# Tiles of one head pair in the attention of a fused kernel: the ninth tile alone, with zeros multiplied at the start and buffers of their own for the last output halves

## The chip, the cores and the metric

The kernel runs on one core of a Trainium2 chip. The metric is the device time of one execution in microseconds, the median of several runs. The core has a matrix engine (TensorE, PE in the profile; its weight loads are shown apart as PEld), a vector engine (VectorE, DVE), an activation engine (ScalarE, ACT), a general engine (GpSimd, POOL) and a queue engine (SyncE, SP) that issues transfers (DMA). The engines run side by side, each through its own instructions in order, and wait for each other by semaphores. SBUF is the working memory with 128 partitions; PSUM is the memory into which TensorE writes.

## The reference

Attention over 8 batches of 8 heads, 576 rows, head dimension 64, in which all scores more than tau below the row's largest are dropped, and then a two-layer network without biases whose nonlinearity is h - tanh(h).

```python
def _attn_ref(q, k, v, tau):                 # q, k, v: (8, 8, 576, 64), tau = 0.02
    scores = (1.0 / np.sqrt(64)) * np.matmul(q, k.transpose(0, 1, 3, 2))
    thresh = np.max(scores, axis=-1, keepdims=True) - tau
    scores = np.where(scores >= thresh, scores, -1000000000.0)
    scores = scores - np.max(scores, axis=-1, keepdims=True)
    attn = np.exp(scores)
    attn = attn / (np.sum(attn, axis=-1, keepdims=True) + 1e-09)
    return np.matmul(attn, v)

def _moe_ref(x, w_in, w_out):                # x: (4608, 512), w_in: (512, 2048), w_out: (2048, 512)
    h = x @ w_in
    g = h - np.tanh(h)
    return g @ w_out

# x is the attention's output, with the heads of one row side by side
```

## The kernel before

Two heads are worked on together as a *pair*; there are 32 pairs, four to a batch. A pair has nine tiles of 128 query rows: four of the first head, four of the second, and one that takes the last 64 rows of both. The program counts tiles through from 0 to 287 and takes one step for each. In a step it computes the scores of the tile eight ahead, shifts and bends the scores of tiles further on, turns one tile's weights (transposes them and takes the exponential), multiplies another's with v, and puts in a piece of the network on a batch that is already attended to.

Two neighbouring tiles are a *duo*: an A and a B, side by side in one buffer of 2 x 576 columns, that is nine blocks of 128. As a pair has nine tiles, the before kernel counts A and B straight through all the pairs. The ninth tile of an even pair is the A of a duo whose B is the shared tile of the next pair, which there comes first:

```python
def kind(i):
    return "AB"[i % 2]

def place(i):
    p, j = divmod(i, TPP)                    # TPP = 9
    j = j - p % 2
    return (p, None, 4) if j in (-1, 8) else (p, j // 4, j % 4)
```

Scores, and their copy to SBUF with the row maximum. The buffer in PSUM is one of two:

```python
def scores(i):
    p, hh, t = place(i)
    ps = ps_big.tile([P, 1024], F32, name="psS", tag="big")
    ...
    if hh is None:                           # rows of both heads: eight matmuls, 64 rows each
        ...
    else:
        lhs = qT[:, (5 * hh + t) * P : (5 * hh + t + 1) * P]
        for n, kk in enumerate((kT, kS)):
            for dst, src in ((main, MAIN[hh]), (rem, REM[hh])):   # 512 and 64 columns
                nc.tensor.matmul(out=ps[:, dst], lhsT=lhs, rhs=kk[:, src],
                                 start=(n == 0), stop=(n == 1))
    sc = sc_pool.tile([P, S], F32, name="sc")
    ...
    nc.vector.tensor_scalar(out=sc, in0=ps[:, lo : lo + S], scalar1=SC, scalar2=None,
                            op0=ALU.mult, op1=ALU.max, accum_out=mx[:, c : c + 1])
```

Once in a duo the maxima are turned into the biases of both tiles. A Prelu with a very steep slope then drops what lies below the threshold. From the seventh pair on, a duo is transposed by a DMA; the first six pairs are transposed on TensorE:

```python
def shift(i):
    if kind(i) == "A":
        return
    ...
    nc.vector.tensor_scalar(out=..., in0=..., scalar1=-1.0, scalar2=tau, op0=ALU.mult, op1=ALU.add)
    nbs[i - 1], nbs[i] = nb[:, 0:1], nb[:, 1:2]

def kink(i):
    ...
    nc.scalar.activation(out=z, in_=sc, func=ACT.Prelu, bias=nb, scale=1.0, alpha=STEEP)
    if on_pe(i):                             # pairs 0 to 5
        zts[i] = zt
    elif kind(i) == "B":
        zts[i] = zt_pool.tile([P, TPP, P], BF16, name="zT")
        nc.sync.dma_start_transpose(out=zts[i], in_=zt)

def weights(i):                              # the branch for pairs 6 to 31
    ...
        pt = p_pool.tile([P, TPP * P], FP16, name="pT")
        nc.scalar.activation(out=pt[:, 0 : n * P], in_=zts.pop(i)[:, 0:n, :], func=ACT.Exp)
```

The weighted sum of a duo. The fifth block holds the last 64 columns of A above the first 64 of B, and one matmul of 130 columns serves both. The two shared tiles in one duo belong to two pairs and are multiplied one pair at a time:

```python
def attend(i):
    ...
    nc.tensor.matmul(out=po[:, t - 1 : t + 1, :], lhsT=pt[:, 4 * P : 5 * P],
                     rhs=vb[:, hh, 4:6, :], start=True, stop=False, ...)
    for n in range(8):
        ab, c = divmod(n, 4)
        blk = 5 * ab + c
        nc.tensor.matmul(out=po[:, t - 1 + ab, :], lhsT=pt[:, blk * P : (blk + 1) * P],
                         rhs=vb[:, hh, c, :], start=False, stop=(n == 7), ...)

def attend_shared(p, ab, pt):                # five matmuls of 130 columns
    for n in range(5):
        blk, c = ((5 * ab + n, n) if n < 4 else (4, 4 + ab))
        nc.tensor.matmul(out=ops[p, 1 - p % 2][:, 4:6, :], lhsT=pt[:, blk * P : (blk + 1) * P],
                         rhs=vb[:, :, c, :], start=(n == 0), stop=(n == 4))
```

The output tiles come from a pool that goes round two buffers. The last row block of the last part is done in two halves of 256 columns, from the same two buffers, so that the stores of the first half can begin earlier:

```python
y_pool = pool("y", 2)

def project(m, ms, part, ps, last, cols=slice(0, d_model)):
    ...
        yo = y_pool.tile([P, nc_], F32, name="yo")
        if last:
            nc.scalar.copy(out=yo, in_=ps)
        else:
            nc.vector.tensor_copy(out=yo, in_=ps)
    # the store of yo is issued after that; for the last part two stores of 64 rows
```

The start: k and q of pair 0 are loaded in pieces, split into a high and a low half on ScalarE, VectorE and GpSimd, and transposed on TensorE. Until the first of them has landed TensorE has nothing to do. GpSimd splits k and q of the later pairs, casts v, makes the shifted copy kS of each kT, and casts the 16 pieces of the two weight matrices in the first seven pairs.

Of the kernel before, what the change touches and what calls it, by code (L numbers as in the profile page):

```python
# [18 lines left out]
def kernel(  # L19
# [27 lines left out]
    NPAIR = B * HPAIR  # L47
    DM_C = d_model // P
    DF_C = d_ff // P


    TPP = 9
    NTILE = NPAIR * TPP

# [16 lines left out]
    NMB = B + 1  # L71

    const = ctx.enter_context(tc.tile_pool(name="const", bufs=1))
    ident_f16 = const.tile([P, P], FP16, name="ident_f16")
    make_identity(nc, ident_f16)
    ident_bf = const.tile([P, P], BF16, name="ident_bf")
# [10 lines left out]
    for i in range(NV):  # L87
        vb = const.tile([P, 2, 6, D + 1], BF16, name=f"vb{i}")
        nc.gpsimd.memset(vb[:, :, 4:6, :], 0.0)
        nc.gpsimd.memset(vb[:, :, 0:4, D : D + 1], 1.0)  # L90
        nc.gpsimd.memset(vb[0:64, :, 4, D : D + 1], 1.0)
        nc.gpsimd.memset(vb[64:P, :, 5, D : D + 1], 1.0)
        vbs.append(vb)


    mx3 = []
# [71 lines left out]
    warm = const.tile([P, 1], F32, name="warm")  # L168
    nc.vector.memset(warm, 0.0)
    nc.scalar.activation(out=warm, in_=warm, func=ACT.Exp)  # L170

    hls = {}

# [109 lines left out]
    REM = (slice(512, 576), slice(576, 640))  # L283
    scs, mxs, nbs, zs, zts, pts, ops = {}, {}, {}, {}, {}, {}, {}

    def kind(i):

        return "AB"[i % 2]

    def place(i):  # L290

        p, j = divmod(i, TPP)
        j = j - p % 2
        return (p, None, 4) if j in (-1, 8) else (p, j // 4, j % 4)

    def scores(i):
        p, hh, t = place(i)
        qT, kT, kS = mats[p, "q"], mats[p, "k"], mats[p, "ks"]
        ps = ps_big.tile([P, 1024], F32, name="psS", tag="big")
        main, rem, lo = slice(0, 512), slice(512, 576), 0  # L300
        if kind(i) == "B":
            main, rem, lo = slice(512, 1024), slice(448, 512), 448
        if hh is None:
            qrem = REM
            if q_by_dma(p):
                qrem = (slice(512, 640, 2), slice(513, 640, 2))
            for n, kk in enumerate((kT, kS)):
                for dst, srcs in ((main, MAIN), (rem, REM)):
                    for hh in range(2):
                        nc.tensor.matmul(  # L310
                            out=ps[64 * hh : 64 * hh + 64, dst],
                            lhsT=qT[:, qrem[hh]], rhs=kk[:, srcs[hh]],
                            start=(n == 0), stop=(n == 1),
                        )
        else:
            lhs = qT[:, (5 * hh + t) * P : (5 * hh + t + 1) * P]
            for n, kk in enumerate((kT, kS)):
                for dst, src in ((main, MAIN[hh]), (rem, REM[hh])):
                    nc.tensor.matmul(  # L319
                        out=ps[:, dst], lhsT=lhs, rhs=kk[:, src],  # L320
                        start=(n == 0), stop=(n == 1),
                    )
        sc = sc_pool.tile([P, S], F32, name="sc")
        if kind(i) == "B":
            mx = mxs[i] = mxs.pop(i - 1)
        else:
            mx = mxs[i] = mx3[i // 2 % len(mx3)]
        c = int(kind(i) == "B")
        nc.vector.tensor_scalar(  # L329
            out=sc, in0=ps[:, lo : lo + S], scalar1=SC, scalar2=None,  # L330
            op0=ALU.mult, op1=ALU.max, accum_out=mx[:, c : c + 1],
        )
        scs[i] = sc

    def shift(i):

        if kind(i) == "A":
            return
        mx = mxs.pop(i)
        nb = st_pool.tile([P, 9], F32, name="nb", tag="nb")  # L340
        nc.vector.tensor_scalar(  # L341
            out=nb.rearrange("p (a b) -> p a b", b=3)[:, :, 0:2],
            in0=mx.rearrange("p (a b) -> p a b", b=4)[:, :, 0:3],
            scalar1=-1.0, scalar2=tau, op0=ALU.mult, op1=ALU.add,
        )
        nbs[i - 1], nbs[i] = nb[:, 0:1], nb[:, 1:2]

    def kink(i):
        sc, nb = scs.pop(i), nbs.pop(i)
        if kind(i) == "B":  # L350
            zt = zs.pop(i - 1)
            z = zt[:, S:W]
        else:
            zt = zs[i] = z_pool.tile([P, W], BF16, name="z")
            z = zt[:, 0:S]
        nc.scalar.activation(  # L356
            out=z, in_=sc, func=ACT.Prelu, bias=nb, scale=1.0, alpha=STEEP
        )
        if on_pe(i):
            zts[i] = zt  # L360
        elif kind(i) == "B":
            zts[i] = zt_pool.tile([P, TPP, P], BF16, name="zT")
            nc.sync.dma_start_transpose(out=zts[i], in_=zt)

    def weights(i):


        kd = kind(i)
        n, off = {"A": (4, 0), "B": (5, 4)}[kd]
        if on_pe(i):  # L370
            z = zts.pop(i)
            pl, tag = (ps_h, "h") if i % 2 and i < HPAIR * TPP else (ps_y, "y")
# [23 lines left out]

    def attend(i):

        if kind(i) == "A":
            return  # L400
        p, hh, t = place(i)
        vb, pt = vbs[p % NV], pts[i]
        if hh is None:

            attend_shared(p - 1, 0, pt)
            return
        if t == 1:
            ops[p, hh] = ps_o.tile([P, 6, D + 1], F32, name="psO", tag="o")
            if p % 2 and hh == 0:
                attend_shared(p, 1, pts.pop(i - 2))  # L410
        po = ops[p, hh]

        nc.tensor.matmul(  # L413
            out=po[:, t - 1 : t + 1, :], lhsT=pt[:, 4 * P : 5 * P],
            rhs=vb[:, hh, 4:6, :], start=True, stop=False, skip_group_check=True,
        )
        for n in range(8):
            ab, c = divmod(n, 4)
            blk = 5 * ab + c
            nc.tensor.matmul(  # L420
                out=po[:, t - 1 + ab, :], lhsT=pt[:, blk * P : (blk + 1) * P],
                rhs=vb[:, hh, c, :], start=False, stop=(n == 7), skip_group_check=True,
            )
        pts.pop(i)

    def attend_shared(p, ab, pt):

        vb = vbs[p % NV]
        for n in range(5):
            blk, c = ((5 * ab + n, n) if n < 4 else (4, 4 + ab))  # L430
            nc.tensor.matmul(
                out=ops[p, 1 - p % 2][:, 4:6, :], lhsT=pt[:, blk * P : (blk + 1) * P],
                rhs=vb[:, :, c, :], start=(n == 0), stop=(n == 4),
            )

    osb = {}

    def norm(p, hh):
        po = ops.pop((p, hh))
        if hh == 0:  # L440
            osb[p] = o_pool.tile([P, 5, 2, D], BF16, name="osb")
        shared = hh != p % 2
        n = 4 + shared
        rc = st_pool.tile([P, 5], F32, name="rc", tag="rc")
        nc.vector.reciprocal(out=rc[:, 0:n], in_=po[:, 0:n, D])
        nc.vector.tensor_tensor(  # L446
            out=osb[p][:, 0:4, hh, :], in0=po[:, 0:4, 0:D],
            in1=rc[:, 0:4].unsqueeze(2).to_broadcast([P, 4, D]), op=ALU.mult,
        )
        if shared:  # L450
            nc.vector.scalar_tensor_tensor(
                out=osb[p][:, 4, :, :], in0=po[:, 4:6, 0:D], scalar=rc[:, 4:5],
                in1=own, op0=ALU.mult, op1=ALU.mult,
# [56 lines left out]
    def project(m, ms, part, ps, last, cols=slice(0, d_model)):  # L510
# [4 lines left out]
            )  # L515
        if part == 3:
            nc_ = cols.stop - cols.start
            yo = y_pool.tile([P, nc_], F32, name="yo")
            if last:
                nc.scalar.copy(out=yo, in_=ps)  # L520
            else:
# [157 lines left out]
    for s in range(-AHEAD, NTILE + LAG + 3):  # L679
# [37 lines left out]
        for i in atts.pop(s, []):  # L717
            pp, jj = divmod(i, TPP)
            if i < NTILE:
                attend(i)  # L720
                odd = pp % 2
                if jj == 3 + odd:
                    norm(pp, 0)
                elif odd and jj in (0, 8):
                    norm(pp - (jj == 0), 1)
            if pp and jj == 1 + pp % 2:
                emit_x(pp - 1)
        for step in plan.pop(s, []):
            step()
# [61 lines left out]
```

## Time and profile before

| | |
|---|---|
| time, median of 3 runs | 540.55 us (540.01 to 540.85) |
| span of the profiled execution | 538.8 us, granted TensorE clock 1.00 |
| TensorE matmul busy | 508.4 us, 94% |
| VectorE busy | 424.5 us, 79% |
| ScalarE busy | 435.2 us, 81% |
| GpSimd busy | 290.2 us, 54% |
| scores copy, L329, 288 times | 753 ns each |
| Prelu, L356, 288 times | 770 ns each |
| Exp of a duo, L392, 117 times | 1153 ns each |
| transposes of z by DMA, L363, 117 times | 3.6 us from issue to landing |
| first matmul on loaded data | 5.42 us from the start |

A group in the profile is all instructions of one line, engine and shape. Its busy time counts overlapping instructions once, and the mean is that of one instruction from its beginning to its end, so neighbours that overlap make the mean larger than the distance between them. A row of the waits reads: who waited, for whom, us in total, how many times, the longest. The chain of work goes back from the last instruction to what released it, and so on to the start. The numbers after L are lines of the kernel.

### The profile page before, as it was taken

What the parts mean: (1) busy time and instruction counts of PE and PEld (TensorE: products, weight loads), DVE (VectorE), ACT (ScalarE), POOL (GpSimd) and SP (SyncE); (2) the same over time, 40 slices, a digit from 0 to 9 for tenths busy, and PEclk for the clock granted to TensorE, in tenths of its full rate; (3) what the DMA queues carried; (4) which work ended last, traced back from release to release, by engine and by line L of the source; (5) the groups of instructions that cost most, each with busy time, mean ns of one, the idle gap of its engine ahead of it and who ended that gap; (6) DMA issues with size and microseconds to landing.
All of it is one profiled execution on the core that took longest, in us unless ns stands there. A gap on an engine that the chain in (4) does not pass through costs nothing.

```text
span 538.8 us, 12796 instructions
## 1 busy us (share of the span) xinstructions
PE 508.4 (94%) x4640; PEld 289.0 (54%) x4640; DVE 424.5 (79%) x1183; ACT 435.2 (81%) x617; POOL 290.2 (54%) x390
## 2 busy tenths in 40 slices
PE   5989899989999999999999899999999999999996
PEld 3666566555555555555555555555455555444444
DVE  4898888988888988888888888898889788554440
ACT  4999899998888998899888988899888989543330
POOL 7999996776555656666645654566665620000000
PEclk9999999999999999999999999999999999999999
DMA  6555657989898999798989889798978986301113
GB/s 209 174 184 151 205 177 141 195 181 183 162 196 157 181 182 199 155 180 183 196 175 183 184 182 189 159 166 195 191 164 176 202 140 116 103 19 41 39 40 79
DMA packets 202687, 85.32 MB, mean 158 GB/s; under 512 B 170240, under 2 KB 195072, under 8 KB 202624
## 3 DMA queue, kind: packets, MB, share of 16 engines
q1 hardware_dynamic: 202032, 84.08, 74.4%
q8 instruction: 36, 0.59, 0.5%
q10 hardware_dynamic: 592, 0.43, 0.3%
q14 instruction: 27, 0.22, 0.1%
HBM read 36.70 MB, written 9.44 MB: 86 GB/s over the span
## 4 chain that ended last, share of the span: by engine, by line
PE 64%; DVE 12%; ACT 8%; POOL 5%; DMA 5%; issue 4%; SPq 1%; DVEq 0%; ACTq 0%; POOLq 0%
PE psY L512 19%; PE psH L486 17%; PE psS L319 14%; ACT z L356 3%; PE psO L420 3%; DVE g L505 3%; DVE sc L329 3%; PE psHt L486 3%; DVE kT L251 2%; ACT pT L392 2%; PE psS L310 2%; PE ps_k L228 2%; DMA qT<-qhl 2%; DVE yo L522 2%; DMA zT<-z 2%
## 5 line engine op out<-in xcount | busy, mean ns | idle before, releaser
L356 ACT ACTIVATE z<-sc,nb 128x576 bf16<-128x576 f32 x288 | 216.9, 770 | 39.0 <-DVE nb L341 38.5
L329 DVE TENSOR_SCALAR_CACHE_REDUCE sc<-psS 128x576 f32<-128x576 f32 x288 | 214.2, 753 | 40.5 <-PE psS L319 29.0
L512 PE MATMUL psY<-w_out_sb,g 128*128 128x512 bf16 (+1 forms) x592 | 145.9, 373 | 0.8 <-DVE yo L522 0.8
L257 POOL COPY kS<-kT 64x1152 f16<-64x1152 f16 x62 | 70.7, 1141 | 131.9 <-DVE kT L251 69.7
L392 ACT ACTIVATE pT<-zT 128x1152 f16<-128x1152 bf16 x117 | 134.9, 1153 | 2.1 <-DMA zT<-z 2.1
L486 PE MATMUL psH<-xT,w_in_sb 128*128 128x512 bf16 x480 | 123.3, 379 | 2.5 <-DVE g L505 2.3
L319 PE MATMUL psS<-kT,qT 128*128 128x512 f16 (+1 forms) x512 | 104.9, 286 | 9.7 <-DVE kT L251 4.9
L319 PEld LDWEIGHTS <-qT 128*128 128x128 f16 x1024 | 74.2, 98 | 65.3 <-issue 13.6
L505 DVE SCALAR_TENSOR_TENSOR g<-th,psH 128x512 bf16<-128x512 f32 x128 | 87.5, 684 | 19.2 <-ACT th L499 18.5
L319 PE MATMUL psS<-kS,qT 128*128 128x512 f16 x496 | 101.4, 286 | 0.0
L499 ACT ACTIVATE th<-psH 128x512 f32<-128x512 f32 x128 | 74.4, 582 | 22.0 <-PE psH L486 22.0
L512 PEld LDWEIGHTS <-g 128*128 128x128 bf16 x592 | 51.0, 98 | 56.8 <-issue 2.4
L486 PEld LDWEIGHTS <-w_in_sb 128*128 128x128 bf16 x576 | 49.8, 98 | 58.2 <-issue 4.7
L420 PE MATMUL psO<-vb,pT 128*128 128x65 bf16 x1024 | 53.3, 194 | 0.0
L420 PEld LDWEIGHTS <-pT 128*128 128x128 f16 x1024 | 44.2, 98 | 9.7
L181 POOL TENSOR_TENSOR qhl<-qraw,qhl 128x576 f16<-128x576 f32 x31 | 39.7, 1280 | 2.7
L181 POOL TENSOR_TENSOR khl<-kraw,khl 128x576 f16<-128x576 f32 x31 | 39.7, 1280 | 2.6
L384 ACT ACTIVATE pT<-psZ 128x512 f16<-128x512 bf16 (+1 forms) x54 | 35.0, 652 | 4.6 <-PE psZ L375 4.0
L522 DVE COPY yo<-psY 128x512 f32<-128x512 f32 (+1 forms) x31 | 21.1, 682 | 14.6 <-DMA out_dram<-yo 6.8
L413 PE MATMUL psO<-vb,pT 128*128 128x130 bf16 x128 | 28.2, 221 | 1.7 <-ACT pT L392 1.5
L251 DVE COPY kT<-ps_k 128x1152 f16<-128x1152 f16 x31 | 23.4, 754 | 7.6 <-PE ps_k L228 7.6
L446 DVE TENSOR_TENSOR osb<-psO,rc 128x256 bf16<-128x256 f32 x64 | 27.2, 424 | 2.2
(76 smaller groups left out, 513.3 us busy)
## 6 DMA issues: line engine op xcount, KB each, us to landing
vraw<-in_v_dram SPq DMA_DIRECT2D x32, 256.0 KB, 3.9
out_dram<-yo SPq DMA_DIRECT2D x32, 256.0 KB, 2.8
kraw<-in_k_dram SPq DMA_DIRECT2D x31, 256.0 KB, 3.3
qraw<-in_q_dram SPq DMA_DIRECT2D x31, 256.0 KB, 3.4
wt<-in_moe_w_in_dram SPq DMA_DIRECT2D x8, 512.0 KB, 4.7
wt<-in_moe_w_out_dram SPq DMA_DIRECT2D x8, 512.0 KB, 3.9
zT<-z SPq DMA_TRANSPOSE x117, 3.6
kraw<-in_k_dram SPq DMA_DIRECT2D x32, 32.0 KB, 3.2
```

The source lines that it names most:

```text
L181: nc.gpsimd.tensor_tensor(out=hl[:, :, 1, :], in0=x, in1=hl[:, :, 0, :], op=ALU.subtract)
L257: nc.gpsimd.tensor_copy(out=o, in_=i)
L319: nc.tensor.matmul(out=ps[:, dst], lhsT=lhs, rhs=kk[:, src], start=(n == 0), stop=(n == 1),)
L329: nc.vector.tensor_scalar(out=sc, in0=ps[:, lo : lo + S], scalar1=SC, scalar2=None, op0=ALU.mult, op1=ALU.max, accum_out=mx[:, c : c + 1],)
L356: nc.scalar.activation(out=z, in_=sc, func=ACT.Prelu, bias=nb, scale=1.0, alpha=STEEP)
L384: nc.scalar.activation(out=pt[:, off * P : (off + n) * P], in_=ps[:, 0 : n * P], func=ACT.Exp)
L392: nc.scalar.activation(out=pt[:, 0 : n * P], in_=zts.pop(i)[:, 0:n, :], func=ACT.Exp)
L420: nc.tensor.matmul(out=po[:, t - 1 + ab, :], lhsT=pt[:, blk * P : (blk + 1) * P], rhs=vb[:, hh, c, :], start=False, stop=(n == 7), skip_gr ...
L486: nc.tensor.matmul(out=ps, lhsT=w_in_sb[:, c, n * P : (n + 1) * P], rhs=xs[m][:, c, :] if m < B else xR[:, c, :, :], start=(c == 0), stop= ...
L499: nc.scalar.activation(out=th, in_=ps, func=ACT.Tanh)
L505: nc.vector.scalar_tensor_tensor(out=gs[m][:, n, :], in0=th, scalar=-1.0, in1=ps, op0=ALU.mult, op1=ALU.add,)
L512: nc.tensor.matmul(out=ps, lhsT=gs[m][:, n, ms * P : (ms + 1) * P], rhs=w_out_sb[:, n, cols], start=(n == 0), stop=(n == DF_C - 1),)
```

## The change

It has three parts. The shared duo is given up: each pair is worked on by itself, with two duos of the first head, the tile of both heads alone as a third kind M in the middle, and two duos of the second head. M has a buffer of five blocks whose last 64 columns are filled once, is transposed and exponentiated alone, and has a shift of its own. The weighted sum of a duo is done one tile at a time in two groups of five matmuls. At the start TensorE multiplies a tile of zeros, so that it is not idle until the first loads land. And the two halves of the last output tile get a buffer each, so that they do not wait for the stores of earlier tiles.

```diff
+    zero = const.tile([P, 512], BF16, name="zero")
+    nc.vector.memset(zero, 0.0)
...
+    NM = 2
+    zms = []
+    for i in range(NM):
+        zm = const.tile([P, 5 * P], BF16, name=f"zm{i}")
+        nc.vector.memset(zm[:, S : 5 * P], -STEEP)
+        zms.append(zm)
...
+    pz = ps_y.tile([P, 512], F32, name="psW", tag="y")
+    for n in range(11):
+        nc.tensor.matmul(out=pz, lhsT=zero[:, 0:P], rhs=zero, start=True, stop=True)
...
-    def kind(i):
-        return "AB"[i % 2]
-    def place(i):
-        ...
+    def kind(j):
+        return "M" if j == 4 else "A" if j in (0, 2, 5, 7) else "B"
...
     def shift(i):
-        if kind(i) == "A":
+        kd = kind(i % TPP)
+        if kd == "A":
             return
...
+        if kd == "B":
+            nbs[i - 1], nbs[i] = nb[:, 0:1], nb[:, 1:2]
+        else:
+            nbs[i] = nb[:, 0:1]
...
     def kink(i):
...
+        else:
+            zt = zms[i // TPP % NM]
             z = zt[:, 0:S]
...
-        elif kind(i) == "B":
+        elif kd != "A":
+            n = 5 if kd == "M" else TPP
             zts[i] = zt_pool.tile([P, TPP, P], BF16, name="zT")
-            nc.sync.dma_start_transpose(out=zts[i], in_=zt)
+            nc.sync.dma_start_transpose(out=zts[i][:, 0:n, :], in_=zt)
...
     def weights(i):
-        n, off = {"A": (4, 0), "B": (5, 4)}[kd]
+        n, off = {"A": (4, 0), "M": (5, 0), "B": (5, 4)}[kd]
...
     def attend(i):
...
+        if kd == "M":
+            pt = pts.pop(i)
+            for c in range(5):
+                nc.tensor.matmul(
+                    out=po[:, 4:6, :], lhsT=pt[:, c * P : (c + 1) * P],
+                    rhs=vb[:, :, c, :], start=(c == 0), stop=(c == 4),
+                )
             return
...
+        for ab in range(2):
+            blocks = [(4 * ab + ab + c, c) for c in range(4)]
+            blocks.append((4, 4 + ab))
+            for n, (blk, c) in enumerate(blocks):
+                nc.tensor.matmul(
+                    out=po[:, (j - 1 - 5 * hh) + ab, :],
+                    lhsT=pt[:, blk * P : (blk + 1) * P], rhs=vb[:, hh, c, :],
+                    start=(n == 0), stop=(n == 4),
+                )
...
-            yo = y_pool.tile([P, nc_], F32, name="yo")
+            yo = y_pool.tile(
+                [P, nc_], F32, name="yo", tag="yo" if nc_ == d_model else f"yo{int(last)}",
+                bufs=2 if nc_ == d_model else 1,
+            )
...
-                if jj == 3 + odd:
-                    norm(pp, 0)
-                elif odd and jj in (0, 8):
-                    norm(pp - (jj == 0), 1)
-            if pp and jj == 1 + pp % 2:
+            if i < NTILE and jj in (4, 8):
+                norm(pp, int(jj > 4))
+            if jj == 1 and pp:
                 emit_x(pp - 1)
```

## The prediction

> **What bounds the kernel now.** I read the table of busy time by stretch first, then the chain of work in order of time, then the waits, and last the timelines of head and tail. The table has a column for each engine (busy us, instructions in brackets). Each row here is one group of four pairs, from the copy that ends one batch's attention to the next:
>
> ```profile
> 182.31:240.81 58.50, 57.22 (x529) 32.25 (x528) 51.06 (x146) 51.94 (x71) 34.48 (x45) 1.00 0.93 181
> 240.81:299.29 58.48, 57.19 (x529) 32.22 (x527) 51.05 (x146) 51.81 (x71) 34.44 (x45) 1.00 0.90 179
> ```
>
> PE is busy 57.2 of 58.5 us, VectorE 51.1, ScalarE 51.9, GpSimd 34.5: in the middle PE has 1.3 us spare in a group, the next two about 7. The chain agrees: in a group it is mostly matmuls in a row, and it shows what each costs there (start, us, what), which is less than the mean of a row of the page, as neighbours overlap.
>
> ```profile
> 308.89 0.86 PE psY L512 x4
> 309.76 0.06 PE psO L413
> 309.81 0.25 PE psO L420 x8
> 310.06 0.49 PE psS L319 x4
> ...
> 312.77 0.29 PE psO L431 x5
> ...
> 323.35 0.61 PE psS L310 x8
> ```
>
> Added up for four pairs: 32 ordinary score tiles at 0.49 are 15.7, 4 shared ones at 0.61 are 2.4, 32 layer steps at 0.86 are 27.5, 16 duos at 0.06+0.25 are 5.0, 4 shared attends at 0.29 are 1.2, six transposed q or k at 0.50 are 3.0, four output transposes at 0.25 are 1.0: 55.8 of 58.5 us. So a step that loads PE counts here, and one that loads ScalarE or VectorE mostly does not.
>
> The first 63 us are different. The waits of GpSimd between 5 and 63 us are one line:
>
> ```profile
> POOL kraw L199 <- DMA kraw<-in_k_dram: 1.2, 1, 1.2
> ```
>
> That is, GpSimd waits once, for the first load, and then never: it works through the splitting of q and k, the casts of v and of the weights, and the shifted copies of k without a gap. The chain leaves it only near 63 us:
>
> ```profile
> 61.17 1.14 POOL kS L257
> 62.36 1.15 POOL kS L257
> 63.51 0.04 issue
> 63.55 0.43 PE psS L310 x3
> ```
>
> ScalarE is close behind it (4.7 to 5.0 us busy of each 5 from 10 to 60 us), and then idles 1.7 us of the five from 60 to 65, when GpSimd's copy is late.
>
> **What the Trainium skill says.** "TensorE: Matmul & The Clock Gate", Part 1 (the HAM clock gate): the array starts at half rate and goes to full rate after some 3.4 us of activity. The trace agrees. Of PE in the head:
>
> ```profile
> 8.00 0.66 PE L319 MATMUL psS<-ksT,qT 128*128 128x512 f16 x2
> 8.47 0.67 PE L319 MATMUL psS<-kT,qT 128*128 128x512 f16 x2
> ...
> 10.75 0.41 PE L319 MATMUL psS<-ksT,qT 128*128 128x512 f16 x2
> 11.00 0.41 PE L319 MATMUL psS<-kT,qT 128*128 128x512 f16 x2
> ```
>
> The same two matmuls (512 and 64 columns) follow each other at 0.47 us at first and at 0.25 after 10.5 us. "ScalarE: Activation LUTs", What ACT_TABLE_LOAD costs: an ACTIVATE with immediate bias takes 186 ns and 0.833 ns an element. For 1152 elements that is 1146; the trace has 1153. It is why a single tile's Exp is dearer per element than half a duo's: for 640 the same rule gives an estimate of 719, and the trace has 704 for an Exp of 640 (there out of PSUM). "DMA: Bandwidth & Descriptors", Anatomy of one DMA: a DMA has about 2 us that do not depend on its size, mostly the receipt of the write. It is stated for the other way of issuing; the 64 KB stores here, from the hardware queues, take 2.0 to 2.2 us to land. That matters for the last tile.
>
> **The change, part by part.**
>
> *No shared duo, TensorE.* A pair has nine tiles in both kernels; the ninth (the 64 left-over rows of each head) was half of a duo with the next pair's, and is now alone. A duo's weighted sum was one matmul of 130 columns and eight of 65; it is now ten of 65. From the chain, 0.25/8 = 0.032 each: ten are 0.316 against 0.06+0.25, so some 0.006 more. Times 128 duos: +0.8 us, on the path. The ninth tile keeps its five matmuls of 130 columns (0.29), its scores (0.61) and, in the first six pairs, its transposes (82 for 81 in two pairs). Nothing else on PE moves.
>
> *ScalarE.* Two pairs had nine Exps of 1152; they now have eight and two of 640. A pair: 4 x 1.153 + 0.704 - 4.5 x 1.153 = +0.127 us, over the 26 pairs that transpose by DMA +3.3 us. Against that, an A tile's Prelu waits for the shift that comes with its partner one step later:
>
> ```profile
> ACT z L356 <- DVE nb L341: 38.5, 58, 1.2
> ```
>
> A tiles go from 144 to 128, and the single tile has its shift a step earlier; in proportion, 38.5 x 16/144 = 4.3 us of this idle time goes. ScalarE comes out about even, with some 6.6 us spare in a group. What can reach PE is where ScalarE is late at the start of a group, when four steps carry no layer work and PE runs ahead. These are the waits of PE's weight load for pT:
>
> ```profile
> PEld L413 <- ACT pT L392: 4.1, 9, 0.7
> ```
>
> The single tile's Exp falls on the fifth step of a group, just behind these four. I allow 0.15 us in each of seven groups: +1.0 us.
>
> *VectorE.* 16 more shifts at 0.150: 2.4 us, beside PE. The pieces of the norms are the same in number.
>
> *DMA.* 130 transposes of z for 117, the 26 single ones of five blocks, not nine: 41 blocks a pair for 40.5, 1.2% more. ScalarE waited for zT 2.1 us in all: no cost.
>
> *Zeros at the head.* Eleven matmuls of 512 columns. At the half rate a 512+64 pair takes 0.47, so one of 512 about 0.42: eleven are 4.6 us if none is at full rate. Beginning at about 1.2 us they end at 5.3 to 5.9, where the first real matmul stood at 5.42. The real ones up to 9.43 then go at full rate: four score pairs at 0.25, not 0.47, save 0.9, the transposes before them 0.3. So PE is 0.7 to 1.2 us earlier at 10 us, and ScalarE's Prelus start that much sooner. But GpSimd starts with its load and has no wait until 63 us; what PE gains is waited away by then. I credit 0.2 us.
>
> *Buffers of the last tile.* The ring of two output tiles made the last half wait:
>
> ```profile
> 532.75 0.37 ACT L520 COPY yo<-psY 128x256 f32<-128x256 f32 x1 [1.12 <-PE psY L512]
> 533.16 2.84 ACTq L531 DMA_DIRECT2D out_dram<-yo  x2
> 535.04 0.42 DVE L522 COPY yo<-psY 128x256 f32<-128x256 f32 x1 [6.80 <-DMA out_dram<-yo]
> ```
>
> Of the 6.80 us idle most is the wait for PE: its last matmuls run from 528.65 for 5.81, to 534.46. The copy could start about 0.1 later and starts at 535.04. The gain is 0.5 us, not 6.8, and it goes straight to the end.
>
> The sum: +0.8 + 1.0 - 0.2 - 0.5 = +1.1 us, from 540.55 to about 541.6.
>
> **The rivals.**
> - *ScalarE becomes the bound.* If all of its +3.3 us reached the end, the time would be 540.55 + 3.3 + 0.8 - 0.7 = 544. For it: ScalarE sits on the chain at every group's start. Against it: its 6.6 us spare in a group, seven times over.
> - *The head gain is real.* If ScalarE, not GpSimd, sets the pace up to 63 us, 1.2 us are won there, and the time is 540.6. For it: ScalarE is 95 to 100% busy there. Against it: the one line of GpSimd's waits.
> - *The shorter waits for the shift win.* If the 4.3 us of idle time were what holds PE at group starts, a third of it would bring the time to about 539.5. Against it: these waits lie beside a busy PE.
> - *The DMA engines.* They are busy 0.90 to 0.96 in the middle. If 13 more transposes made each wait of ScalarE for zT longer (3.6 us is the median to landing, 6.3 the longest), one late Exp in a group of 0.5 us would add 3.5, to 545. Against it: 1.2% more blocks, and five steps of about 1.7 us between issue and use.
>
> **Range and chances.** The terms are each about 1 us, and of both signs; the largest single rival is +3.3 us. With the best two of head, tail and shift together it could go to 538.8, with ScalarE or the DMA engines at work to 545. For 2% it would take 10.8 us: nearly 1.5 us in every group, more than any term found. So faster by over 2% has 0.01, slower 0.03.
>
> **What would show it right or wrong.** The table by stretch: a group of four pairs should last 58.6 to 59.0 us with PE at 57.3. Exps of 640 should stand at about 0.70, duos at 0.32 on the chain. The wait of z for nb should fall to some 34 us. In the head the score matmuls should go at 0.25 from the first, ScalarE's first Prelu move from 11.5 to about 10.5, yet GpSimd's copy at 61 to 63 us stay where it is. The last VectorE copy should start 0.1 us after the last matmul. The prediction is wrong if GpSimd's copies move forward in the head, if PE's waits for pT grow beyond 10 us, or if waits for zT appear in every group.

## The result and the profile after

The changed kernel takes 537.01 us (median; 535.75 to 537.74) where the kernel before, beside it on the same chip, takes 540.31 (539.57 to 540.91). The ratio is 0.9937, with a 95% interval of 0.9922 to 0.9951: it is faster by about 3.3 us. The prediction was 541.6, with a range from 538.8, so the result lies outside the range, and on the other side of the time before.

The table of busy time by stretch, of the kernel after: start:end and length, busy us of PE, PEld, VectorE, ScalarE and GpSimd (instructions in brackets), clock, DMA share, GB/s. Each row is a group of four pairs, as in the prediction (two of the four in the middle are shown):

```profile
182.20:240.17 57.97, 57.28 (x543) 31.87 (x542) 51.28 (x148) 52.28 (x73) 34.47 (x45) 1.00 0.88 184
240.17:298.13 57.96, 57.27 (x543) 31.88 (x542) 51.27 (x147) 52.27 (x73) 34.43 (x45) 1.00 0.91 184
```

PE is busy 57.3 us, 0.1 more than before, as predicted. But the group is shorter, and all are alike. Before they were not; the third group of that kernel, which the prediction did not show, is the longest:

```profile
299.29:358.46 59.17, 57.48 (x530) 32.30 (x528) 51.12 (x145) 52.17 (x72) 34.69 (x45) 1.00 0.92 181
```

Four groups in a row last 58.50, 58.48, 59.17 and 58.76 before, 57.97, 57.96, 57.97 and 57.99 after: 234.91 against 231.89, so 3.0 us of the 4.8 by which the two profiled executions differ (538.8 and 534.0). The first 182 us give 0.1 of it, what follows the fourth group 1.7. A profile is one execution; the medians differ by 3.3.

The groups became shorter where PE was idle. The waits of PE from 120 to 420 us (who, for whom, us in total, times, longest), first before, then after. Both are complete but for idle times under 0.15 us, which these lists leave out:

```profile
PE psS L319 <- DVE kT L251: 3.7, 5, 1.2
PE psH L486 <- DVE g L505: 1.6, 5, 0.3
PE psO L413 <- ACT pT L392: 1.5, 4, 0.4
PE psS L310 <- DVE sc L329: 0.9, 1, 0.9
PE psS L310 <- DMA qT<-qhl: 0.7, 2, 0.4
```

```profile
PE psS L327 <- DVE sc L337: 2.1, 11, 0.3
PE psH L495 <- DVE g L514: 1.6, 5, 0.3
```

Before, PE waits once in every group for VectorE's copy of the transposed keys, kT, and nearly as often for the exponential pT. After, neither is listed, and waits for sc, VectorE's copy of the scores, take the place of a part of them. The wait for kT is the largest, and the prediction did not speak of it.

One group without a disturbance shows the trade, before (240.81 to 299.29 us) and after (240.17 to 298.13 us):

```profile
PE psS L319 <- DVE kT L251: 0.5, 1, 0.5
PE psO L413 <- ACT pT L392: 0.4, 1, 0.4
PE psH L486 <- DVE g L505: 0.3, 1, 0.3
```

```profile
PE psS L327 <- DVE sc L337: 0.4, 2, 0.2
PE psH L495 <- DVE g L514: 0.3, 1, 0.3
```

What stands ahead of kT on VectorE is seen in the timeline of both at the start of a group (start, us, engine, line, operation; in brackets the idle time before it). Before:

```profile
302.16 0.57 ACT L499 ACTIVATE th<-psH 128x512 f32<-128x512 f32 x1
...
302.74 1.03 PE L486 MATMUL psH<-xT,w_in_sb 128*128 128x512 bf16 x4
302.76 0.69 DVE L505 SCALAR_TENSOR_TENSOR g<-th,psH 128x512 bf16<-128x512 f32 x1 [0.44 <-ACT th L499]
303.37 0.18 DVE L445 RECIPROCAL rc<-psO 128x4 f32<-128x4 f32 x1
303.58 0.42 DVE L446 TENSOR_TENSOR osb<-psO,rc 128x256 bf16<-128x256 f32 x1
303.92 0.75 DVE L251 COPY kT<-ps_k 128x1152 f16<-128x1152 f16 x1
...
304.72 0.41 PE L319 MATMUL psS<-kT,qT 128*128 128x512 f16 x2 [0.96 <-DVE kT L251]
```

After:

```profile
300.25 0.57 ACT L508 ACTIVATE th<-psH 128x512 f32<-128x512 f32 x1
...
300.88 0.68 DVE L514 SCALAR_TENSOR_TENSOR g<-th,psH 128x512 bf16<-128x512 f32 x1
...
301.38 1.03 PE L495 MATMUL psH<-xT,w_in_sb 128*128 128x512 bf16 x4
301.47 0.75 DVE L264 COPY kT<-ps_k 128x1152 f16<-128x1152 f16 x1
...
302.24 0.45 PE L429 MATMUL psO<-vb,pT 128*128 128x130 bf16 x5
...
302.53 0.41 PE L327 MATMUL psS<-kT,qT 128*128 128x512 f16 x2
...
302.87 0.19 DVE L454 RECIPROCAL rc<-psO 128x5 f32<-128x5 f32 x1
```

Three things differ. Before, the first head's norm (RECIPROCAL and TENSOR_TENSOR) stands between g and kT and puts kT off by 0.55 us (from 303.37 to 303.92). After, kT stands right behind g and the norm follows it. Second, before, VectorE itself is held up 0.44 us here by a late tanh of ScalarE. That is not the rule: it happens in two of the five groups (1.1 us in all), where PE then waits 1.19 and 0.96 us for kT; in the other three VectorE does not wait for tanh, and PE waits 0.51 to 0.52. Third, after, PE has the ninth tile's five matmuls (L429) to do between the layer's step (L495) and the scores, 0.29 us from 302.24 to 302.53; before, the scores come straight after the layer's step. In the kernel before the scores start 0.80 us after the copy of kT begins (303.92 to 304.72), in the kernel after 1.06 (301.47 to 302.53): kT is there 0.26 us before PE gets to it.

The rest went as the prediction had it. The chain of work of the kernel after shows a duo at 0.32 and the ninth tile at 0.61 and 0.29:

```profile
309.04 0.32 PE psO L440 x10
309.35 0.49 PE psS L327 x4
309.84 0.86 PE psY L521 x4
...
313.98 0.61 PE psS L317 x8
...
317.74 0.29 PE psO L429 x5
```

In the head of the kernel after the zeros run from 1.18 us and the scores follow each other at 0.25 from the first:

```profile
1.18 4.48 PE L183 MATMUL psW<-zero 128*128 128x512 bf16 x11 [1.18 <-DVE zero L73]
...
7.34 0.42 PE L327 MATMUL psS<-kT,qT 128*128 128x512 f16 x2 [0.38 <-ACT qT L290]
7.59 0.41 PE L327 MATMUL psS<-ksT,qT 128*128 128x512 f16 x2
```

The first Prelu starts at 10.19, not 11.47. Yet GpSimd's copies at the end of the head stand in the chain where they stood (61.17 and 62.36 before):

```profile
61.24 1.14 POOL kS L270
...
62.43 1.15 POOL kS L270
```

The end of the kernel after, from its timeline:

```profile
524.65 5.60 PE L521 MATMUL psY<-w_out_sb,g 128*128 128x512 bf16 x41
...
530.28 0.42 DVE L534 COPY yo<-psY 128x256 f32<-128x256 f32 x1 [6.25 <-PE psY L521]
```

The last copy follows the last matmul (524.65 + 5.60 = 530.25) by 0.03 us; before it was 0.58.

### The profile page after: what moved, and what is told of

Read it like the earlier page. It is cut to its first block, busy times and chain, and to the rows that moved or that the text cites. A ratio compares the mean times of both kernels' runs of the same rounds, so it can differ in the third digit from the quotient of the medians.

```text
span 534.0 us, 13042 instructions
## 1 busy us (share of the span) xinstructions
PE 512.9 (96%) x4782; PEld 287.9 (54%) x4782; DVE 427.2 (80%) x1202; ACT 438.2 (82%) x630; POOL 290.0 (54%) x390
## 4 chain that ended last, share of the span: by engine, by line
PE 69%; DVE 15%; POOL 7%; ACT 3%; issue 2%; DMA 2%; SPq 0%; DVEq 0%; POOLq 0%; ACTq 0%
PE psY L521 21%; PE psH L495 18%; PE psS L327 14%; DVE sc L337 7%; PE psO L440 5%; DVE g L514 3%; PE psS L317 3%; PE psHt L495 3%; PE ps_k L241 2%; POOL kS L270 2%; DVE kT L264 2%; ACT pT L403 1%; ACT z L374 1%; DVE yo L534 1%; POOL w_in_sb L628 1%
## 5 line engine op out<-in xcount | busy, mean ns | idle before, releaser
L374 ACT ACTIVATE z<-sc,nb 128x576 bf16<-128x576 f32 x256 | 193.4, 768 | 19.7 <-DVE nb L354 19.7
L411 ACT ACTIVATE pT<-zT 128x1152 f16<-128x1152 bf16 (+1 forms) x130 | 138.9, 1068 | 0.4 <-DMA zT<-z 0.4
L495 PE MATMUL psH<-xT,w_in_sb 128*128 128x512 bf16 x480 | 124.0, 379 | 2.3 <-DVE g L514 2.3
L327 PEld LDWEIGHTS <-qT 128*128 128x128 f16 x1024 | 72.3, 97 | 55.7 <-issue 8.7
L495 PEld LDWEIGHTS <-w_in_sb 128*128 128x128 bf16 x576 | 49.2, 98 | 58.2 <-issue 4.5
L440 PEld LDWEIGHTS <-pT 128*128 128x128 f16 x1280 | 55.7, 98 | 25.2 <-issue 1.9
L440 PE MATMUL psO<-vb,pT 128*128 128x65 bf16 x1280 | 61.2, 193 | 0.0
L403 ACT ACTIVATE pT<-psZ 128x640 f16<-128x640 bf16 (+1 forms) x54 | 35.4, 658 | 5.8 <-PE psZ L394 5.4
L354 DVE TENSOR_SCALAR nb<-mx 128x6 f32<-128x6 f32 (+1 forms) x160 | 24.5, 153 | 2.3
```

The costliest lines, as they stand in the source:

```text
L327: nc.tensor.matmul(out=ps[:, dst], lhsT=lhs, rhs=kk[:, src], start=(n == 0), stop=(n == 1),)
L403: nc.scalar.activation(out=pt[:, off * P : (off + n) * P], in_=ps[:, 0 : n * P], func=ACT.Exp)
L440: nc.tensor.matmul(out=po[:, (j - 1 - 5 * hh) + ab, :], lhsT=pt[:, blk * P : (blk + 1) * P], rhs=vb[:, hh, c, :], start=(n == 0), stop=(n ...
L495: nc.tensor.matmul(out=ps, lhsT=w_in_sb[:, c, n * P : (n + 1) * P], rhs=xs[m][:, c, :] if m < B else xR[:, c, :, :], start=(c == 0), stop= ...
```

## The experiments

Two theories of where the time came from. **The norm's place**: the norm of the first head of an even pair moves from the fourth step of its pair to the fifth, because it now takes in the ninth tile, and so comes behind the copy of kT that PE needs at the group's start. **ScalarE**: with the shift of the ninth tile a step earlier and fewer A tiles waiting for their partner, ScalarE is less late at the group's start, and with it tanh, g, kT and pT. "Before" and "after" name the two kernels of this document; each ratio is to the kernel before.

### The three parts alone

Zeros alone, in before:

```diff
+    zero = const.tile([P, 512], BF16, name="zero")
+    nc.vector.memset(zero, 0.0)
+    pz = ps_y.tile([P, 512], F32, name="psW", tag="y")
+    for n in range(11):
+        nc.tensor.matmul(out=pz, lhsT=zero[:, 0:P], rhs=zero, start=True, stop=True)
```

> The kernel before with the zeros at the head and nothing else. If GpSimd sets the pace up to 63 us, the head's gain is waited away: 540.1 to 540.5 against 540.3. If ScalarE sets it, the 1.3 us by which its first Prelu comes sooner reaches the end: about 539.

Measured: 539.92 us, ratio 0.9999 (0.9990 to 1.0009). The zeros bring nothing.

Buffers of their own alone, in before:

```diff
-            yo = y_pool.tile([P, nc_], F32, name="yo")
+            yo = y_pool.tile([P, nc_], F32, name="yo", bufs=2 if nc_ == d_model else 1,
+                             tag="yo" if nc_ == d_model else f"yo{int(last)}")
```

> The kernel before with buffers of their own for the last two half tiles and nothing else. The last VectorE copy should start within 0.1 us of the last matmul and not 0.6 after it: 0.5 us less, about 539.8. If the wait for the store was only a name on a wait for PE, no difference.

Measured: 539.36, ratio 0.9991 (0.9983 to 1.0000), that is 0.5 us, with an interval that reaches 1. The last copy starts at 534.04, 0.03 behind the last matmul.

The shared duo given up alone, that is after without the two parts above:

```diff
-    zero = const.tile([P, 512], BF16, name="zero")
...
-        nc.tensor.matmul(out=pz, lhsT=zero[:, 0:P], rhs=zero, start=True, stop=True)
...
+            yo = y_pool.tile([P, nc_], F32, name="yo")
```

> The changed kernel without its zeros and without the own buffers: the shared duo alone is given up. If this part is what makes the change faster (groups of 58.0 us and not 58.5 to 59.2), 537.3 to 538.0. If the two small parts carry the gain, 540 or more, as the prediction had it for this part (+1.8).

Measured: 537.17, ratio 0.9947 (0.9933 to 0.9961). The product of the three ratios is 0.9937, which is the ratio of the whole change. So giving up the shared duo brings some 2.9 us, and the prediction had put it at a cost of 1.8.

### The norm's place

In before, with its shared duo, only the first head's norm in even pairs is issued later in the same step, behind what prepares the next pair (and so behind kT):

```diff
-                if jj == 3 + odd:
+                if jj == 3 and not odd:
+                    late.append(pp)
+                elif jj == 4 and odd:
                     norm(pp, 0)
...
         for step in plan.pop(s, []):
             step()
+        while late:
+            norm(late.pop(0), 0)
```

> The kernel before, in which the norm of an even pair's first head is put behind the copy of kT of the same step on VectorE, where it stood ahead of it. Theory N (the changed kernel wins because that norm comes one step later and no longer holds up kT, for which PE waits 0.5 to 1.0 us in every group): 1.5 to 3 us less, 537.5 to 539. Theory S (it wins because ScalarE's Exps fall differently, so that tanh and pT come sooner): within 0.5 of 540.3.

Measured: 537.94, ratio 0.9958 (0.9942 to 0.9974). In its timeline the copy follows g, and the scores follow with no idle time shown:

```profile
300.64 0.69 DVE L505 SCALAR_TENSOR_TENSOR g<-th,psH 128x512 bf16<-128x512 f32 x1
...
301.25 0.75 DVE L251 COPY kT<-ps_k 128x1152 f16<-128x1152 f16 x1
301.92 0.17 DVE L445 RECIPROCAL rc<-psO 128x4 f32<-128x4 f32 x1
302.05 0.41 PE L319 MATMUL psS<-kT,qT 128*128 128x512 f16 x2
```

Its waits of PE from 120 to 420 us, complete:

```profile
PE psS L310 <- DMA qT<-qhl: 2.2, 2, 1.2
PE psO L413 <- ACT pT L392: 1.8, 5, 0.4
PE psH L486 <- DVE g L505: 1.6, 5, 0.3
```

The wait for kT (3.7 us) is gone from the list and that for pT is not. The scores still start 0.80 us after the copy of kT begins (301.25 to 302.05): kT comes just in time here, and 0.26 us early in after. The order of two small operations is worth 0.4% by itself, with not one instruction taken out.

The same with the buffers of their own, which makes before into a kernel that still has the shared duo, but has the norm behind kT and the buffers:

```diff
+                if jj == 3 and not odd:
+                    late.append(pp)
...
+                             tag="yo" if nc_ == d_model else f"yo{int(last)}")
```

> The kernel before, shared duo kept, with the norm behind kT and the own buffers for the last halves. If the two add up (2.0 and 0.6): 537.3, the time of the changed kernel, and then giving up the shared duo is worth nothing in itself. If giving it up has a worth of its own beyond the norm's place, this stays 0.5 us or more above the changed kernel, which is 537.0.

Measured: 537.35, ratio 0.9950 (0.9933 to 0.9968). It overlaps with that of after: the shared duo can stay, and nearly the whole gain is had.

The other way round, in after, kT is prepared one step later, to bring it behind the norm:

```diff
-        (5, lambda p: turn(p, "k")),
+        (4, lambda p: turn(p, "k")),
```

> The changed kernel with the transposes of k, and with them the copy of kT, one step later, so that on VectorE the norm of the first head stands ahead of kT again, as in the kernel before. Theory N: the gain is undone in part or whole, 538.5 to 541 against 537.1. If the place of the norm was not what counted, or there is slack of a whole step in kT: within 0.5 of 537.1.

Measured: 538.26, ratio 0.9964 (0.9955 to 0.9972). It is some 1.4 us behind after (0.27% by the ratios), but PE does not wait for kT in it; what it has is one wait of 1.9 us for q's transpose, and groups of 58.2. It says nothing on the norm.

So the norm itself was moved in after: that of the four whole tiles is cut off and done a step earlier, ahead of kT as in before.

```diff
-            if i < NTILE and jj in (4, 8):
+            if i < NTILE and jj == 3 and pp % 2 == 0:
+                norm_four(pp)
+            elif i < NTILE and jj == 4 and pp % 2 == 0:
+                norm_ninth(pp)
+            elif i < NTILE and jj in (4, 8):
                 norm(pp, int(jj > 4))
```

> The changed kernel with the norm of the first head's four tiles cut off from the ninth's in even pairs and put a step earlier, ahead of the copy of kT on VectorE, as it stood in the kernel before. Theory N: PE's waits for kT come back, some 0.5 us in most groups: 1.5 to 2.5 us above its partner behind kT. If the place does not matter once the shared duo is gone, the two are within 0.5 of each other.

Measured: 537.49, ratio 0.9956 (0.9942 to 0.9970), some 1 us behind after, with intervals that overlap. The list of PE's waits from 120 to 420 us has no row for kT. But that list leaves out idle times under 0.15 us, and the timeline at the start of a group shows that PE waits:

```profile
302.53 0.17 DVE L452 RECIPROCAL rc<-psO 128x4 f32<-128x4 f32 x1
...
303.08 0.75 DVE L264 COPY kT<-ps_k 128x1152 f16<-128x1152 f16 x1
303.30 0.45 PE L429 MATMUL psO<-vb,pT 128*128 128x130 bf16 x5
303.88 0.41 PE L327 MATMUL psS<-kT,qT 128*128 128x512 f16 x2
```

The norm puts the copy off by 0.55 us, as in before (302.53 to 303.08), and the scores again start 0.80 us after the copy begins. From the first of the ninth tile's matmuls to the scores it is 0.58 us, where it is 0.29 in after: PE is put off by 0.29 us. It is so at the start of each group from 128 us on, and a group lasts 58.16 us (241.04 to 299.20) against 57.96. So the norm's place counts in the changed kernel too, but for less. Of the 0.55 us, the 0.26 by which kT is early in after is not felt, and without the ninth tile's matmuls at this spot the scores would stand 0.29 us earlier and would wait for all of it. A kernel with these matmuls elsewhere was not run.

The same cut, with the four tiles' part behind kT:

```diff
+            if i < NTILE and jj == 3 and pp % 2 == 0:
+                late.append(pp)
...
+        while late:
+            norm_four(late.pop(0))
```

> The same cut of the norm, with the four tiles' part in the same step but behind the copy of kT. It has 16 reciprocals more than the changed kernel, about 3 us of VectorE that should lie beside PE: within 0.7 of 537.0.

Measured: 540.28, ratio 1.0006 (0.9997 to 1.0014). A new wait would explain most of it. From PE's waits in the same stretch:

```profile
PE psO L429 <- DVE nb L354: 2.2, 5, 0.5
```

The ninth tile's matmuls write the same psO that the late norm still reads (the profile names nb, which stands beside it): 0.44 us in each group, 3.1 in seven. The pair of these two kernels therefore does not isolate the order; the comparison with after does, but for the 16 reciprocals that the cut adds.

### ScalarE's order and load

In before, tanh goes ahead of the Prelus of its step, so that it, g and kT come earlier:

```diff
+        bend()
         for i in kinks.pop(s, []):
             kink(i)
-        bend()
```

> The kernel before with tanh ahead of the two Prelus of a step on ScalarE. VectorE waits for tanh just ahead of the norm and kT (0.44 us at the start of a group), so theory S, that a late ScalarE is behind the gap, has 0.5 us in each of seven groups: 537 to 538.5. Theory N alone: within 1 of 540, as the norm still stands ahead of kT; and z comes later, which may cost as much.

Measured: 545.24, ratio 1.0109 (1.0082 to 1.0135). Its two longest waits of PE from 120 to 420 us:

```profile
PE psS L310 <- DMA qT<-qhl: 7.4, 8, 1.6
PE psS L319 <- DVE kT L251: 2.1, 5, 0.4
```

The wait for kT is 2.1 us, not much less than in the runs with the zeros alone (2.8) and the buffers alone (2.4), which leave the middle as it is; a wait for the transposes of q stands ahead of it. In SyncE's queue all but one of these come right behind a transpose of z, and the edit puts z behind tanh. They also take longer from issue to landing: 4.0 us in the median and 5.7 at most, against 3.6 and 4.9 in before. Which of the two makes PE wait was not tried by itself.

The same in after:

```diff
+        bend()
         for i in kinks.pop(s, []):
             kink(i)
-        bend()
```

> The same in the changed kernel, where PE hardly waits any more (0.7 us in a group). Theory N: no gain left, within 0.7 of 537.1. Theory S: 535.5 to 536.5.

Measured: 541.03, ratio 1.0014 (1.0005 to 1.0023): 4 us lost. Its later groups are like those of after (58.09 and 58.0); the loss is in pairs 5 to 10, with one wait of 2.5 us for q's transpose. In after, tanh last in its step:

```diff
-        bend()
         for i in wts.pop(s, []):
             weights(i)
+        bend()
```

> The changed kernel with tanh behind the Exp of a step, not between Prelu and Exp. Tanh ahead of both cost 4 to 5 us in both kernels. If that was z being late (and the transposes behind it), tanh last brings nothing more or a little: 536 to 537.2. If it was the exponentials being late, the same. If VectorE's g, which waits for tanh, then holds up the scores: 538 to 541.

Measured: 538.10, ratio 0.9960 (0.9948 to 0.9972): some 1.2 us behind after, with PE's waits in the middle as there. Both places of tanh are worse than the one it had.

Next the waits of z for nb, which fell from 38.5 to 19.7 us. If they counted, doing the Prelu concerned one step later, when its nb is there, would bring the gain in before. First for one tile in each group:

```diff
-            kinks.setdefault(... i - MASK, []).append(i)
+            kinks.setdefault(... i - MASK + (i >= 54 and i % 36 == 4), []).append(i)
```

> The kernel before; of each group of four pairs one Prelu, that of the fifth tile (an A), moves one step later, next to its B's, so that ScalarE does tanh and an Exp in the step in which it waited for the bias. Theory S (ScalarE is late at the start of a group for this wait; tanh, g and kT follow): PE's wait for kT goes though the norm still stands ahead of it, 1 to 2.5 us less: 537.5 to 539.2. Theory N alone: within 0.5 of 540.2.

Measured: 541.05, ratio 1.0015 (1.0005 to 1.0024). PE still waits 2.6 us for kT and 2.2 for pT from 120 to 420 us. Then for all A tiles from the seventh pair on:

```diff
-            kinks.setdefault(... i - MASK, []).append(i)
+            kinks.setdefault(... i - MASK + (i >= 54 and kind(i) == "A"), []).append(i)
```

> The kernel before with the Prelus of all A tiles from the seventh pair on one step later, beside their B's. ScalarE's waits for the bias (38.5 us in all) should all but vanish. Theory S: at least as good as the run with one tile, 537 to 539. If ScalarE's idle time counts only at the group's start, the same as that run; if two Prelus in one step make tanh late, worse than before.

Measured: 544.38, ratio 1.0091 (1.0062 to 1.0121). ScalarE's longest wait from 120 to 420 us and PE's in this kernel:

```profile
ACT th L499 <- PE psH L486: 31.4, 51, 1.4
```

```profile
PE psS L310 <- DMA qT<-qhl: 7.1, 7, 1.3
```

The waits for nb (33.8 us in this stretch before) are all gone and 31.4 us of waiting for PE stand in their place: ScalarE had that time to spare, and it waits elsewhere. But the loss lies mostly in the waits for q. In the two groups that have none, from 125.46 to 241.41 us, PE does not wait for pT either, and they last 57.95 and 58.00 us, half a microsecond less than before; the next three last 60.2 to 60.5. So the waits for the bias may stand behind the wait for pT. This edit with q's transposes moved forward, which would tell, was not run. The same edit in after:

```diff
+            ... i - MASK + (i >= 54 and kind(i % TPP) == "A")
```

> The changed kernel with the Prelus of all A tiles one step later in the same way. PE has 0.7 us of gaps left in a group and does not wait for kT: 536.3 to 537.5. If two Prelus in one step make tanh late: 538 or more.

Measured: 537.42, ratio 0.9954 (0.9938 to 0.9969), an interval that overlaps with that of after. In the changed kernel these waits have nothing left to give.

Last, less work for ScalarE at the group's start in before. Two Exps in each group take five blocks, not nine, and their second tile is multiplied with the blocks of the first. So the exponentials of eight blocks in each group are left out, and the output is not the reference's; the instructions and their order stay:

```diff
+            if i % 36 in (1, 3):
+                n = 5
...
+            if i % 36 in (1, 3) and not on_pe(i):
+                blk = c
```

> The kernel before, leaving work out: in every group of four pairs from the seventh pair on the Exps of the first two duos do 640 of 1152 elements, and the second tile of each of these duos is multiplied with the first tile's weights, so its output is not the reference's. TensorE and VectorE do as many instructions as before, in the same order, the norm ahead of kT. ScalarE has 0.86 us less ahead of the tanh for which VectorE's g waits. If ScalarE's lateness is the second condition, PE's wait for kT falls from 0.5 to 1.0 us in a group to near nothing and the time by 1.5 to 3: 537.3 to 538.8. If the norm's place alone makes kT late: within 0.6 of 540.2.

Measured: 538.22, ratio 0.9959 (0.9944 to 0.9973). Its two longest waits of PE from 120 to 420 us:

```profile
PE psS L319 <- DVE kT L251: 2.6, 6, 0.5
PE psS L310 <- DMA qT<-qhl: 1.9, 3, 0.9
```

PE's wait for pT is gone (and its weight load's falls from 4.1 to 2.0), as ScalarE is earlier. That for kT is 2.6, within the 2.4 to 3.7 of the kernels whose middle is that of before: with the norm still ahead of the copy, 0.4 us in a group without a disturbance are left of 0.5. This is the mirror of the norm moved behind kT, where the wait for kT went and that for pT stayed. There are two waits, with a cause each.

### The transposes of q

As PE's waits for q's transposes were what a later ScalarE cost, q was split and transposed one step earlier, on top of the moved norm and the buffers:

```diff
-        (8, lambda p: split(p, "k")),
-        (7, lambda p: split(p, "q")),
+        (9, lambda p: split(p, "k")),
+        (8, lambda p: split(p, "q")),
...
-        d = 5 if q_by_dma(p) else 3 - (p == 1)
+        d = 6 if q_by_dma(p) else 3 - (p == 1)
```

> The kernel before with the norm behind kT, the own buffers, and q and k split one step earlier so that the transposes of q by DMA are issued a step earlier. In the run without this last edit PE waited 2.6 us in all for these transposes between 120 and 420 us, 1.4 of it once; the changed kernel hardly did. If that wait is what is left between the two, it goes: 536 to 537. If GpSimd, which then has k and q a step sooner, only moves the wait elsewhere: 537.4.

Measured: 536.46, ratio 0.9926 (0.9907 to 0.9946). The same edit in after:

```diff
+        (9, lambda p: split(p, "k")),
+        (8, lambda p: split(p, "q")),
...
+        d = 6 if q_by_dma(p) else 3 - (p == 1)
```

> The changed kernel with the same earlier split and transpose of q. Its profile shows 0.4 us of PE waiting for q: 536.5 to 537.2 against 537.0. If the wait for q comes and goes from one execution to the next (its six runs reach from 535.8 to 537.7), the median falls to about 536.

Measured: 535.76, ratio 0.9914 (0.9901 to 0.9927): the lowest median of this study, 1.2 us under that of after. Alone, in before:

```diff
+        d = 6 if q_by_dma(p) else 3 - (p == 1)
```

(with the two lines of the splits as above)

> The kernel before with the earlier split of q and k and the earlier transpose of q alone; shared duo, norm ahead of kT and the ring of two buffers as they were. If the wait for q is a loss of its own beside the norm's, it is worth what it brought on top of the norm and the buffers (0.9): 539.3 against 540.3. If it appears only because the norm's loss is gone, no difference.

Measured: 540.10, ratio 0.9990 (0.9980 to 0.9999). PE still meets the waits for kT (2.9 us from 120 to 420) and pT (1.9), and no longer one for q. So an earlier q brought 0.1% here and 0.2% in each of the two kernels without the wait for kT; why it brings less here is not shown.

## Why the prediction was wrong

**The step that failed** is "I allow 0.15 us in each of seven groups: +1.0 us", together with the sentence on which VectorE was dismissed, "The pieces of the norms are the same in number". The number is about the same (the norm now also covers the ninth tile); the place is not, and I did not look where it moves. In a group PE's idle time did not grow by 0.15 us but fell: PE has 1.3 to 1.7 us a group in which it is not busy before, and 0.7 after. Of this the wait for kT is 3.7 us over five groups, 0.7 each, and that for pT 1.5, 0.3 each. I had read the weight load's waits for pT and gave the change a cost there; the first row of PE's own waits, for kT, I left out, though it is PE's longest in the middle. And "Nothing else on PE moves" holds for the load, not for the place: the ninth tile's five matmuls moved to where PE would otherwise wait for kT.

**What is shown.** The wait for kT is the norm's place in the kernel before: moving the norm alone removes it and brings 0.42%, where giving up the shared duo brings 0.53%. The wait for pT is ScalarE's lateness: lightening ScalarE alone removes it and leaves 0.4 us of the wait for kT in a group. The changed kernel has neither. The norm's place counts there as well, for some 1 us in all and 0.29 us at the start of each group; the ninth tile's matmuls fill the rest of that wait.

In groups without a disturbance the parts add up. Such a group lasts 58.48 us before, 57.94 with the norm moved (239.55 to 297.49 us), 58.06 with ScalarE lightened (239.81 to 297.87) and 57.96 in the changed kernel. The two alone bring 0.54 and 0.42, together 0.96. The changed kernel brings 0.52, since PE has 0.1 us more to do in it and waits 0.4 for sc, which neither of the other two does.

**What stays open.** Which of the pieces takes the wait for pT away in the changed kernel was not tried by itself: its ScalarE has no less to do, but fewer A tiles that wait for their bias. Two more pieces moved a step earlier with the change, the norm of the second head of even pairs and the output transposes of these pairs; neither was tried alone. And the first 182 us, with the first two of the seven group starts, gain only 0.1 us.

**The rest of the sum.** Ten matmuls a duo at 0.32: right, PE +0.1 us a group. The wait of z for nb: "some 34" was 19.7 (why more than in proportion was not looked into). The rival that built on it, "The shorter waits for the shift win", came nearest the measured time. Its sum is off by itself (a third of 4.3 us off 541.6 is 540.2, and without the +1.0 it is 539.2, not 539.5), and whether its reason is right stays open: doing all those Prelus later costs 0.9% in before, but by waits for q, and takes half a microsecond off the groups without them. Exps of 640 at "about 0.70": the transposed ones take 0.726. Waits for zT: 2.1 us fell to 0.4, so a cost of the DMA engines did not come. The zeros: 0.2 credited, none measured, with GpSimd's copies at 61 and 62 us unmoved, as argued. The buffers: 0.5, as measured. On the Trainium skill: its activity rule for the clock ("TensorE: Matmul & The Clock Gate", Part 1 (the HAM clock gate)) held here too, as eleven zero matmuls over 4.48 us brought the first scores to full rate. That this was worth nothing (0.9999) fits GpSimd as the head's bound.

**The sum put right**: +0.8 (PE) - 3.7 (group starts, what is left of the 2.9 net) + 0 (zeros) - 0.5 (buffers) = -3.4, against 3.3 measured. The -3.7 is worked back from the measured total, and would be 0.53 us in each of seven groups; in the profiled executions the first two of them gain almost nothing and the next four 3.0 us.

## What to carry to other kernels

Where the busiest engine still has a microsecond spare in each round, list its own waits first, longest first, and ask of each what stands ahead of its releaser in that engine's order, and what the busiest engine itself has to do until it needs the result: 0.29 us of its own matmuls hid a part of the same wait here, and what was left was too short for the list of waits. A change that leaves the number of operations alone can still move a small one past a copy that another engine waits for: here 0.6 us of normalizing, moved by itself behind such a copy, was worth 0.4%. And when an engine that feeds a DMA queue is moved later, look at the next user of that queue: here its transfers, moved forward a step, brought 0.2% where the wait for kT was gone. The two moves together were not run.

## What the runs showed of the hardware that was not expected

Moving tanh ahead by one place in ScalarE's order cost 5 us, and it came out largely on another engine: as eight waits of PE, 7.4 us together, for transposes of q, which stand in SyncE's queue behind those of z and took 4.0 us to land in the median, not 3.6. And the zeros showed what a 512-column matmul costs before the rate has risen: with the zeros alone, eleven take 4.88 us, 0.44 each, where four take 0.86, 0.215 each, later on. In the kernel after, eleven take 4.48, as the last of them are faster.
